# Means' rows by DMA, weight sums from step 16 on, and another place for the third product in a fused attention and feed-forward kernel

## The chip, the cores and the metric

The kernel runs as one launch on one core of a Trainium2 chip. A core has TensorE (PE in the profile; PEld is its weight load), VectorE (DVE), ScalarE (ACT), GpSimd (POOL) and SyncE (SP), which here issues every DMA. Each engine works through its own instructions in the order in which the program was written and waits on semaphores for the others. The metric is the device time of one execution in microseconds. Before the change it is 620.76 us, the median of three runs (620.72 to 621.04).

## The reference, cut to what matters

```python
# attention: 4 batches, 8 heads, 768 positions, 64 values a head; blocks of 32, window of 16
k_sum = k.reshape(B, H, nb, 32, D).max(axis=3)        # maxima of the keys of a block
v_sum = v.reshape(B, H, nb, 32, D).mean(axis=3)       # means of the values of a block
scores = concat(where(|i-j| < 16, q k^T / 8, -1e9), q k_sum^T / 8 + log(32))
x = softmax(scores) @ concat(v, v_sum)                 # 3072 tokens x 512
# feed-forward
h = x @ w_in                                           # 512 -> 2048
g = h * tanh(softplus(h))                              # Mish
out = g @ w_out                                        # 2048 -> 512
```

Inputs and output are float32.

## The kernel before

The kernel fuses both. Tokens go in six groups of 512 (g = 0 to 5), the hidden width in 16 slices of 128 (fc), so there are 96 steps (g, fc), numbered i = 16 g + fc. A matrix product in float32 is made of three products of rounded parts (upper x upper, upper x lower, lower x upper), so each weight and each activation exists as an upper and a lower part; the split is an upper copy on ACT (`ah`, L532) and a subtraction on DVE (`al`, L534).

**Attention** is done in 48 units (c, hp): 256 queries of one pair of heads. A unit has scores on PE (`att_scores`, L359), maxima on DVE (`att_maxima`, L380), exponentials on ACT (L393), divisors on DVE (L407, L408), the normalization on POOL (L412), a transpose on PE (L418) with a copy by ACT (L422), the product with the values on PE (L444) and, for later groups, a copy of the result by ACT into `x_blocks` (L483). For each unit SP loads the queries and keys into `qk` (L319) and the values into `vw` (L335). Both hold room for 24 rows or columns of block summaries: POOL copies the key maxima into `qk` (L324) and the value means into the last 24 rows of `vw`, four times side by side (L336). The maxima and means of a batch are made on DVE (`key_summary` L284, `value_means` L309) from sources which SP loads (L243, L247), and the means are laid out by a small DMA (`value_summary`, L315).

**Steps 0 to 18** are written out by hand as a list of words (`order`): `ph16` is the first layer's product of step 16, `po15` the second layer's of step 15, `al14` the lower part of step 14, `oc0` the copy of two of group 0's four finished output blocks from PSUM, and so on. In this stretch the weights are loaded as well and turned into float32 parts: five DVE instructions (L176 to L197) and two ACT instructions for each piece of 128 x 1024.

**Steps 19 to 31** run in a loop. Beside the steps, DVE makes what the last four groups need: there the first layer takes seven products for two slices instead of eight, and the factors are sums and differences of quarters of the weights. `weight_sums` puts them into a list of waiting DVE work: for pair p of slices `first_sums(p)` (L743 to L746, L733, L734) and `second_sums(p)` (L752, L733, L734), both in a work area called `results`, from which SP sends the parts to DRAM (`w_sums`, L721). `fill(us)` hands DVE as much of the waiting work as fits. Before the change pair 0 is made at the end of step 19, and pairs 1 to 5 from step 20 to 29, a half at each step. The same area is where ACT and DVE put finished output blocks (`ff_store`, L563), which SP stores (L564).

**Steps 32 to 63** go in pairs (`ff_in_pair`): the seven products 1 to 7 (six matmuls of 256 columns each, L806) into two PSUM tiles, `one` and `two`; `chain` is the left half of `one`, `other` the left half of `two`. Between the products ACT copies intermediate sums out (L813, L818, L819, L823), DVE adds (L816, L824, L831), and at the end ACT applies Mish (L829, L830, L832). The order on PE is: products 1, 2, 5, 6; half of the second layer of the pair before; product 7; the other half; products 4 and 3. `chain` holds product 1, then 6, 7 and 4 on top of one another; ACT copies it out after 1, after 6 and after 7. `other` holds product 5, which L819 copies out, and then product 3 is added on top of it. DVE adds the second layer's weight sums in the same stretch (L768 to L777). `load_sums` brings the sums of the pair after next from DRAM (L793, 1024 KB and 768 KB). The batch's maxima and means for the last batch are made after a pair's odd step, in `loads`.

**Steps 64 to 95** use the seven products in both layers and no attention.

Of the kernel before, what the change touches and what calls it, by code (L numbers as in the profile page):

```python
# [9 lines left out]
F32 = mybir.dt.float32  # L10
# [10 lines left out]
P = 128  # L21
# [36 lines left out]
MORE = (3.0, 2.5, 2.0, 3.0)  # L58
# [15 lines left out]
def fused_kernel(ctx: ExitStack, tc: tile.TileContext, q0, qk, kt, v0, vw, vs, w_in, w_out, out):  # L74
# [477 lines left out]
    stores = []  # L552

# [4 lines left out]
    def ff_store(g, *tokens):  # L558
        if not res:
            res.append(stage_words("results"))  # L560
        for t in tokens:
            o = res[0].rearrange("p (t f) -> p t f", t=TG // P)[:, t, :]
# [6 lines left out]


# [54 lines left out]
    def summary_of(name):  # L625
# [18 lines left out]
        "lvw": of_unit(att_load_values),  # L644
    }

# [18 lines left out]
        G15 al15 T16 ph17 pc17 al14 lqk19 kc19 X17 pc16 mi16 po14 po15 xh17 ah16 mi17 ah17 ph18 al16 oc0 oc1 mi18 X16  # L665
# [27 lines left out]
    dram = ctx.enter_context(tc.tile_pool(name="dram", bufs=1, space=bass.MemoryType.DRAM))  # L693
    kept = [dram.tile([P, 2, 7, CH], F32, name=f"w_sums_{p}") for p in range(NFC // 2)]
    kept_out = [dram.tile([P, 2, 3 * CH], F32, name=f"w_out_sums_{p}") for p in range(NFC // 2)]
# [5 lines left out]
    area = res[0]  # L701

    def home(p):
        k = 2 * p
        name, k = ("w_early", k) if k < EARLY else ("w_late", k - EARLY)
        t = grounds[name]
        n = t.shape[1] // 2
        return [t[:, part * n + k * WP:part * n + (k + 2) * WP] for part in range(2)]

    unsent = []  # L710

    def send():
        while unsent:
            unsent.pop(0)()

    def quarters(t):
        return t.rearrange("p (b f) -> p b f", f=CH)

    def keep(p, part, first, t):
        n = t.shape[1]  # L720
        unsent.append(lambda: nc.sync.dma_start(kept[p][:, part, first:first + n, :], t.bitcast(F32)))  # L721
        if p > 5:
            send()

    def keep_blocks(p):
        for part, t in enumerate(home(p)):
            for first, blocks_ in ((0, quarters(t[:, :2 * CH])), (2, quarters(t[:, 3 * CH:]))):
                keep(p, part, first, blocks_)

    def split_sums(p, first, whole, upper):  # L730
        whole = quarters(whole)
        hi, lo = upper.bitcast(F32R), whole.bitcast(F32R)
        return [(0.45, lambda: nc.vector.tensor_copy(hi, whole)),  # L733
                (0.7, lambda: nc.vector.tensor_sub(lo, whole, hi.bitcast(F32))),  # L734
                (0, lambda: (keep(p, 0, first, upper), keep(p, 1, first, whole)))]

    def first_sums(p):

        hi, lo = home(p)
        w, t = area[:, :2 * WP], area[:, 2 * WP:3 * WP]  # L740
        a11, a12, a21, a22 = (w[:, k * CH:(k + 1) * CH] for k in range(4))
        s1, s2 = t[:, :CH], t[:, CH:]
        return [(0, send), (1.25, lambda: nc.vector.tensor_add(w, hi.bitcast(F32), lo.bitcast(F32))),  # L743
                (0.45, lambda: nc.vector.tensor_add(s1, a21, a22)),
                (0.45, lambda: nc.vector.tensor_sub(s2, s1, a11)),
                (0.45, lambda: nc.vector.tensor_sub(a22, a12, s2))] + split_sums(  # L746
                    p, 3, t, quarters(area[:, 3 * WP:]))

    def second_sums(p):
        w = area[:, :2 * WP]  # L750
        a11, a21 = w[:, :CH], w[:, WP:3 * CH]
        made = [(0.45, lambda: nc.vector.tensor_sub(a21, a11, a21))]  # L752
        return made + split_sums(p, 5, w[:, WP:], quarters(w[:, :WP]))
# [9 lines left out]
    def out_sums(p):  # L763
        k = p % 2 if p < 5 else 0
        w = area[:, k * 2 * WP:(k + 1) * 2 * WP]
# [6 lines left out]
        hi = grounds["w_late"][:, (1 + k) * 4 * WP:][:, :2 * WP] if p < 5 else area[:, 2 * WP:].bitcast(F32R)  # L772
# [93 lines left out]
    def loads(i):  # L866
# [7 lines left out]
        for f, b, hp in sorted(chain.get(i, ()), key=in_order):  # L874
            f(b, hp)

# [460 lines left out]
```

## Time and profile before

| | |
|---|---|
| median of three runs | 620.76 us (620.72 to 621.04) |
| profiled execution, its own time | 620.96 us |
| span of its instructions | 619.0 us |
| mean granted TensorE clock | 0.996 |
| PE busy | 595.2 us (96%) |
| DVE busy | 461.1 us (74%) |
| ACT busy | 389.6 us (63%) |
| POOL busy | 114.6 us (19%) |
| DMA | 158.75 MB, mean 256 GB/s |

The span is the time from the first to the last instruction that the profile holds; the execution's own time holds 1.96 us more. Busy is the time in which an engine had an instruction under way. Numbers before an instruction are microseconds from the span's start; in brackets behind it stands the idle time of its engine just before it and who ended that.

### The profile page before, as it was taken

The page shows a single profiled execution, that of the slowest core. Times are in us where ns is not written, and L with a number is a line of the kernel's source. Part 1 is how long each engine was busy: PE and PEld are TensorE (multiplying, and loading weights), DVE is VectorE, ACT ScalarE, POOL GpSimd, SP SyncE. Part 2 cuts the span into 40 slices and gives each one's busy share as a digit, 9 for nine tenths or more (in the row PEclk, how much of TensorE's full clock was granted, in tenths as well). Part 3 has the DMA queues.
Part 4 walks back from the last instruction along what each step waited for, and adds up shares of the span by engine and source line. Part 5 has one row for each costly group of instructions (what it writes and reads, how often), then busy time and mean ns, then how long its engine had stood idle before and what let it go on. Part 6 is the DMA issues. An engine that isn't in the chain of part 4 may idle for free.

```text
span 619.0 us, 13932 instructions
## 1 busy us (share of the span) xinstructions
PE 595.2 (96%) x5142; PEld 527.4 (85%) x5142; DVE 461.1 (74%) x1158; ACT 389.6 (63%) x990; POOL 114.6 (19%) x159
## 2 busy tenths in 40 slices
PE   3899999999999998999999999999999999999997
PEld 3787777778788887888888889888889999999997
DVE  3999999995489758668695466888668777675564
ACT  3987576776446635577858785776446566755662
POOL 3642212322023112122222231322000000000000
PEclk9899999999999999999999999999999999999999
DMA  9977567661388888599988868686869989898853
GB/s 274 252 242 268 192 199 246 204 208 47 123 272 281 265 285 296 180 360 333 370 264 284 280 214 294 237 289 238 297 244 342 301 291 318 278 316 290 292 185 105
DMA packets 66644, 158.75 MB, mean 256 GB/s; under 512 B 9616, under 2 KB 18832, under 8 KB 66576
## 3 DMA queue, kind: packets, MB, share of 16 engines
q1 hardware_dynamic: 66576, 157.85, 75.5%
q8 instruction: 41, 0.67, 0.5%
q14 instruction: 27, 0.22, 0.1%
HBM read 130.42 MB, written 27.26 MB: 255 GB/s over the span
## 4 chain that ended last, share of the span: by engine, by line
PE 54%; DVE 18%; ACT 7%; DMA 7%; issue 2%; SPq 1%; POOL 0%; DVEq 0%; POOLq 0%; ACTq 0%
PE po L544 13%; PE m L1010 12%; PE inner L1112 12%; PE ph L806 9%; PE ph L516 3%; DMA vsum<-vs 3%; DMA qk<-qk 2%; ACT pr L393 2%; DVE al L534 2%; PE x_ps L444 2%; ACT L393 1%; PE pt_ps L418 1%; PE sc L359 1%; DVE w L180 1%; DMA w_sums<-results 1%
## 5 line engine op out<-in xcount | busy, mean ns | idle before, releaser
L412 POOL TENSOR_TENSOR pr<-pr,rs 128x480 f32<-128x480 f32 x48 | 58.7, 1224 | 258.0 <-DVE rs L408 216.6
L393 ACT ACTIVATE pr<-pr,nm 128x120 f32<-128x120 f32 x192 | 73.6, 386 | 18.7 <-DVE nm L380 18.5
L544 PE MATMUL po<-w_early_out_hi,al 128*128 128x512 f32 x160 | 62.7, 392 | 2.3 <-DVE al L534 2.3
L544 PE MATMUL po<-w_early_out_hi,ah 128*128 128x512 f32 x160 | 64.2, 401 | 0.0
L544 PE MATMUL po<-w_early_out_lo,ah 128*128 128x512 f32 x160 | 62.2, 389 | 0.0
L516 PE MATMUL ph<-xh,w_early_in 128*128 128x512 f32 x160 | 52.0, 391 | 0.0
L806 PE MATMUL ph<-xh,w_early_in 128*128 128x256 f32 x272 | 50.9, 279 | 0.7 <-ACT x_blocks L483 0.4
L1112 PE MATMUL inner<-xh,w_early_in 128*128 128x256 f32 x240 | 49.2, 279 | 0.0
L806 PEld LDWEIGHTS ph<-xh,w_early_in 128*128 128x128 f32 x272 | 42.7, 187 | 2.1 <-ACT h L813 0.8
L534 DVE TENSOR_TENSOR al<-h,ah 128x512 fp32r<-128x512 f32 x32 | 22.4, 709 | 26.0 <-ACT ah L532 26.0
L1112 PEld LDWEIGHTS inner<-xh,w_early_in 128*128 128x128 f32 x240 | 39.5, 187 | 0.1
L544 PE MATMUL po<-w_late_out_hi,ah 128*128 128x512 f32 x96 | 38.8, 404 | 0.0
L544 PEld LDWEIGHTS po<-w_early_out_hi,al 128*128 128x128 f32 x160 | 30.1, 188 | 9.0 <-DVE al L534 4.5
L380 DVE CUSTOM_DVE_ANT_0 pr<-sc,base 128x120 f32<-128x120 f32 x128 | 31.3, 276 | 8.6 <-PE sc L359 8.6
L544 PE MATMUL po<-w_late_out_lo,ah 128*128 128x512 f32 x96 | 37.5, 390 | 0.1
L806 PE MATMUL ph<-xl,w_early_in 128*128 128x256 f32 x136 | 37.4, 275 | 0.0
L336 POOL COPY vw<-vm 24x512 f32<-24x512 f32 x40 | 31.8, 817 | 29.7 <-PE x_ps L444 15.2
L544 PE MATMUL po<-w_late_out_hi,al 128*128 128x512 f32 x96 | 37.2, 388 | 0.0
L523 ACT ACTIVATE a<-ph 128x512 f32<-128x512 f32 x32 | 19.0, 599 | 28.0 <-PE ph L516 27.2
L393 ACT ACTIVATION_READ_ACCUMULATOR pr<-pr,nm 128x1 f32 x192 | 36.3, 189 | 0.0
L544 PEld LDWEIGHTS po<-w_early_out_hi,ah 128*128 128x128 f32 x160 | 30.0, 188 | 6.5 <-issue 1.6
L516 PEld LDWEIGHTS ph<-xh,w_early_in 128*128 128x128 f32 x160 | 30.0, 188 | 6.1
(269 smaller groups left out, 1754.1 us busy)
## 6 DMA issues: line engine op xcount, KB each, us to landing
w_early_in<-w_sums SPq DMA_DIRECT2D x32, 1024.0 KB, 7.5
w_early_in<-w_sums SPq DMA_DIRECT2D x32, 768.0 KB, 9.1
qk<-qk SPq DMA_DIRECT2D x40, 496.0 KB, 7.4
w<-w_in SPq DMA_DIRECT2D x16, 512.0 KB, 5.1
w<-w_out SPq DMA_DIRECT2D x16, 512.0 KB, 4.0
w_sums<-results SPq DMA_DIRECT2D x32, 256.0 KB, 3.0
vw<-vw SPq DMA_DIRECT2D x40, 192.0 KB, 3.9
w_late_in<-w_out_sums SPq DMA_DIRECT2D x25, 256.0 KB, 3.2
```

The source lines that it names most:

```text
L336: nc.gpsimd.tensor_copy(vwt[KW:KA], summary[b, hp][1].unsqueeze(1).broadcast_to([NB, NQ, P]))
L380: nc.vector.tensor_tensor_reduce(out=pr[:, j, :], in0=ps[h][:, at + pair * KA:at + (pair + 1) * KA], in1=m, scale=-SCALE, scalar=-NEG, op0 ...
L393: nc.scalar.activation(pr[:, s, :], pr[:, s, :], AF.Exp, scale=-1.0, bias=nm[:, s:s + 1], accum_out=sm[:, s:s + 1])
L412: nc.gpsimd.tensor_mul(u["p"], u["p"], u["r"].unsqueeze(2).broadcast_to([P, NQ, KA]))
L444: nc.tensor.matmul(x, u["v"][0:rows, s, d], pt, start=(c >= CG), stop=(c >= CG or s == NQ - 1))
L516: nc.tensor.matmul(turned(ph), w[:, cc * P:(cc + 1) * P], turned(x[:, cc, :]), start=(cc == 0 and n == 0), stop=(cc == NCC - 1 and n == 2))
L523: nc.scalar.activation(a, st[g, fc], AF.Mish)
L534: return lambda: nc.vector.tensor_sub(al, a, ah.bitcast(F32))
L544: nc.tensor.matmul(turned(po[g][t]), a[:, tok], turned(w), start=(fc == 0 and n == 0), stop=(fc == NFC - 1 and n == 2))
L806: nc.tensor.matmul(turned(ps), w_[:, a * P:(a + 1) * P], turned(x[:, a, :]), start=(begins and a == 0 and n == 0), stop=(a == 1 and n == 2 ...
L1010: nc.tensor.matmul(turned(ps), a_[:, tok], turned(w_), start=(begins and n == 0), stop=(n == 2), skip_group_check=True)
L1112: nc.tensor.matmul(turned(ps), w_[:, a * P:(a + 1) * P], turned(x[:, a, :]), start=(begins and a == 0 and n == 0), stop=(a == 1 and n == 2 ...
```

## The change

1. The means' rows of `vw` are written by a DMA on SP's queue instead of a copy on POOL.
2. The weight sums of pair 0 are made in the written order, as the words `W0a` (behind `al14`) and `W0b` (behind `po15`); those of pairs 1 to 5 come two steps earlier each (at the ends of steps 18 to 27). Their helper functions move up in the file unchanged, and the work area is fetched when first asked for. The first two loads of sums are issued at steps 25 and 30 instead of 25 and 27.
3. In `ff_in_pair` product 3 stands next to product 7, its addition next to the addition of 7, and the Mish of the first slice comes first.
4. For the last batch, maxima and means are made in the middle of the next pair, ahead of the filled-in work there, which gets 1 us less in such a pair.
5. `load_sums` of the pair after next is cut in two: products 1, 2, 4, 5 where it was, products 6, 7, 3 behind the loads of queries and keys.
6. In pairs without scores the third and fourth share of filled-in work are swapped.

```diff
-MORE = (3.0, 2.5, 2.0, 3.0)
+MORE = (3.0, 2.5, 3.0, 2.0)
...
-        nc.gpsimd.tensor_copy(vwt[KW:KA], summary[b, hp][1].unsqueeze(1).broadcast_to([NB, NQ, P]))
+        nc.sync.dma_start(vwt[KW:KA], summary[b, hp][1].unsqueeze(1).broadcast_to([NB, NQ, P]))
...
+    def sums_now(name):
+        p, second = int(name[:-1]), name[-1] == "b"
+        if not second:
+            keep_blocks(p)
+        for _, f in (second_sums if second else first_sums)(p):
+            f()
+        send()
...
-        G15 al15 T16 ph17 pc17 al14 lqk19 kc19 X17 pc16 mi16 po14 po15 xh17 ah16 mi17 ah17 ph18 al16 oc0 oc1 mi18 X16
+        G15 al15 T16 ph17 pc17 al14 W0a lqk19 kc19 X17 pc16 mi16 po14 po15 W0b xh17 ah16 mi17 ah17 ph18 al16 oc0 oc1 mi18 X16
...
-    def load_sums(pair):
+    def load_sums(pair, parts=(slice(0, 4), slice(4, 7))):
         if pair < (NG - WHOLE) * NFC // 2:
-            for some in (slice(0, 4), slice(4, 7)):
+            for some in parts:
...
         product(7, chain)
+        product(3, other)
         nc.scalar.copy(second[:, low], chain)
         nc.vector.tensor_add(second[:, high], second[:, low], second[:, high])
+        nc.vector.tensor_add(first_[:, high], other, first_[:, high])
         spread[1]()
         between[1]()
         product(4, chain)
-        product(3, other)
+        nc.scalar.activation(first_, first_, AF.Mish)
+        nc.scalar.activation(second[:, low], chain, AF.Mish)
         nc.scalar.activation(second[:, high], second[:, high], AF.Mish)
-        nc.scalar.activation(second[:, low], chain, AF.Mish)
-        nc.vector.tensor_add(first_[:, high], other, first_[:, high])
-        nc.scalar.activation(first_, first_, AF.Mish)
...
-    def loads(i):
+    def loads(i, pair=None):
...
-        for f, b, hp in sorted(chain.get(i, ()), key=in_order):
+        if pair is not None:
+            load_sums(pair, [slice(4, 7)])
+        if i < whole_steps:
+            summaries(i)
+
+    def summaries(i):
+        some = sorted(chain.pop(i, ()), key=in_order)
+        for f, b, hp in some:
             f(b, hp)
+        return some
...
-    order_of_sums = {20 + k: (k // 2 + 1, k % 2) for k in range(10)}
+    order_of_sums = {18 + k: (k // 2 + 1, k % 2) for k in range(10)}
...
-        if i == done:
-            keep_blocks(0)
-            put_first(0, first_sums(0) + second_sums(0))
...
+    weight_sums(done - 1)
+    fill(8)
...
-        if whole_steps - i in (7, 5):
+        if i in (25, 30):
             send()
-            load_sums(3 - (whole_steps - i) // 2)
+            load_sums(int(i == 30))
...
-                   [lambda: (second_exponents(0), fill(slots[0], i + 0.3)), lambda: (second_exponents(1), norms(i), fill(slots[1], i + 0.6))])
+                   [lambda: (second_exponents(0), fill(slots[0] - (summaries(i - 1) + summaries(i) != []), i + 0.3)), lambda: (second_exponents(1), norms(i), fill(slots[1], i + 0.6))])
...
-        load_sums(pair + 2)
+        load_sums(pair + 2, [slice(0, 4)])
...
-        loads(i + 1)
+        loads(i + 1, pair + 2)
```

## Rows read from the trace of the kernel before

**Rows 1.** Busy time in two stretches: us, then PE, PEld, DVE, ACT, POOL (instructions).
```profile
40.00:134.00 94.00, 89.56 (x637) 70.80 (x634) 90.79 (x159) 63.54 (x121) 24.60 (x20) 1.00 0.63 205
134.00:245.00 111.00, 111.00 (x746) 90.84 (x745) 79.42 (x198) 59.34 (x145) 22.33 (x27) 1.00 0.68 224
```

**Rows 2.** Waits of PE and PEld, whole span: us in total, times, longest.
```profile
PE pt_ps L418 <- POOL pr L412: 4.9, 3, 1.9
...
PEld ph L806 <- ACT h L813: 0.8, 3, 0.3
...
PEld ph L806 <- ACT x_blocks L483: 0.6, 1, 0.6
```

**Rows 3.** Timeline, POOL's first, second and last L336 of 40 to 134, DVE beside them.
```profile
55.07 1.49 POOL L336 COPY vw<-vm 24x512 f32<-24x512 f32 x1
56.01 1.10 DVE L534 TENSOR_TENSOR al<-a,ah 128x512 fp32r<-128x512 f32 x1
...
70.32 0.96 POOL L336 COPY vw<-vm 24x512 f32<-24x512 f32 x1
69.33 1.48 DVE L176 TENSOR_SCALAR w<-w 128x1024 uint32<-128x1024 uint32 x1
70.73 1.09 DVE L534 TENSOR_TENSOR al<-a,ah 128x512 fp32r<-128x512 f32 x1
...
128.19 2.44 POOL L336 COPY vw<-vm 24x512 f32<-24x512 f32 x2 [7.28 <-PE ph L516]
130.08 1.12 DVE L176 TENSOR_SCALAR w<-w 128x1024 uint32<-128x1024 uint32 x1
```

**Rows 4.** Source line L176: minimum, median and maximum of its sixteen instructions in ns.
```profile
L176 DVE TENSOR_SCALAR w<-w x16: 680/691/1483, 17.2 to 139.8; 128x1024 uint32<-128x1024 uint32 x16
```

**Rows 5.** DMA issues: tiles, count, KB each, median us to landing.
```profile
w_sums<-results SPq DMA_DIRECT2D x32, 256.0 KB, 3.0
```

**Rows 6.** Timeline from 154 to 162 us, DVE, ACT, PE.
```profile
154.27 0.69 DVE L534 TENSOR_TENSOR al<-a,ah 128x512 fp32r<-128x512 f32 x1 [4.64 <-ACT ah L532]
...
155.91 0.58 ACT L563 COPY results<-po 128x512 f32<-128x512 f32 x1
...
161.18 0.49 PE L544 MATMUL po<-w_early_out_hi,ah 128*128 128x512 f32 x1
```

**Rows 7.** Timeline from 172 to 179 us, DVE: pair 0's sums, first and last instruction.
```profile
172.96 1.21 DVE L743 TENSOR_TENSOR results<-w_early_in 128x1024 f32<-128x1024 f32 x1
...
178.10 0.69 DVE L734 TENSOR_TENSOR results<-results 128x512 fp32r<-128x512 f32 x1
```

**Rows 8.** Timeline from 236 to 248 us, DVE and PE.
```profile
236.62 1.23 DVE L743 TENSOR_TENSOR results<-w_late_in 128x1024 f32<-128x1024 f32 x1 [1.61 <-DMA w_sums<-results]
...
240.20 0.28 DVE L380 CUSTOM_DVE_ANT_0 pr<-sc,first 128x120 f32<-128x120 f32 x1
...
247.72 0.65 PE L418 MATMUL pt_ps<-ident,pr 128*120 128x128 f32 x4 [1.76 <-POOL pr L412]
```

**Rows 9.** Timeline from 254 to 256 us, DVE and PE.
```profile
254.18 0.42 DVE L816 TENSOR_TENSOR h<-ph,h 128x256 f32<-128x256 f32 x1
...
255.33 1.71 PE L806 MATMUL ph<-w_early_in 128*128 128x256 f32 x12 [0.79 <-ACT h L823]
```

**Rows 10.** Timeline round 266 us: DVE, ACT and PE in the second pair.
```profile
264.22 0.92 DVE L284 TENSOR_REDUCE spare<-ks 128x24 f32<-128x768 f32 x1
...
266.70 0.37 ACT L819 COPY h<-ph 128x256 f32<-128x256 f32 x1 [1.26 <-DVE h L816]
...
266.23 0.89 PE L806 MATMUL ph<-w_early_in 128*128 128x256 f32 x6
```

**Rows 11.** Timeline round 458 us, ACT and PE: the last pair.
```profile
458.13 0.37 ACT L819 COPY h<-ph 128x256 f32<-128x256 f32 x1 [0.54 <-DVE h L816]
...
458.37 0.84 PE L806 MATMUL ph<-w_early_in 128*128 128x256 f32 x6
```

**Rows 12.** Timeline at 430 us, ACT.
```profile
430.94 0.63 ACT L832 ACTIVATE h<-h 128x512 f32<-128x512 f32 x1 [3.74 <-DVE h L831]
```

More of the change, by code (lines that the diff above doesn't have):

```diff
@@ L552, in fused_kernel @@
     stores = []
+    unsent = []
     def store():
@@ L558, in ff_store @@
     def ff_store(g, *tokens):
-        if not res:
-            res.append(stage_words("results"))
         for t in tokens:
-            o = res[0].rearrange("p (t f) -> p t f", t=TG // P)[:, t, :]
+            o = area().rearrange("p (t f) -> p t f", t=TG // P)[:, t, :]
             (nc.vector.tensor_copy if t % 2 else nc.scalar.copy)(o, po[g][t])
@@ L568, in ff_store, with area, home @@
                 put_out()
+    dram = ctx.enter_context(tc.tile_pool(name="dram", bufs=1, space=bass.MemoryType.DRAM))
+    kept = [dram.tile([P, 2, 7, CH], F32, name=f"w_sums_{p}") for p in range(NFC // 2)]
+    kept_out = [dram.tile([P, 2, 3 * CH], F32, name=f"w_out_sums_{p}") for p in range(NFC // 2)]
+    def area():
+        if not res:
+            res.append(stage_words("results"))
+        return res[0]
+    def home(p):
+        k = 2 * p
+        name, k = ("w_early", k) if k < EARLY else ("w_late", k - EARLY)
+        t = grounds[name]
+        n = t.shape[1] // 2
+        return [t[:, part * n + k * WP:part * n + (k + 2) * WP] for part in range(2)]
@@ new lines, in send, with quarters, keep, keep_blocks @@
+    def send():
+        while unsent:
+            unsent.pop(0)()
+    def quarters(t):
+        return t.rearrange("p (b f) -> p b f", f=CH)
+    def keep(p, part, first, t):
+        n = t.shape[1]
+        unsent.append(lambda: nc.sync.dma_start(kept[p][:, part, first:first + n, :], t.bitcast(F32)))
+        if p > 5:
+            send()
+    def keep_blocks(p):
+        for part, t in enumerate(home(p)):
+            for first, blocks_ in ((0, quarters(t[:, :2 * CH])), (2, quarters(t[:, 3 * CH:]))):
+                keep(p, part, first, blocks_)
@@ new lines, in split_sums, with first_sums @@
+    def split_sums(p, first, whole, upper):
+        whole = quarters(whole)
+        hi, lo = upper.bitcast(F32R), whole.bitcast(F32R)
+        return [(0.45, lambda: nc.vector.tensor_copy(hi, whole)),
+                (0.7, lambda: nc.vector.tensor_sub(lo, whole, hi.bitcast(F32))),
+                (0, lambda: (keep(p, 0, first, upper), keep(p, 1, first, whole)))]
+    def first_sums(p):
+        hi, lo = home(p)
+        w, t = area()[:, :2 * WP], area()[:, 2 * WP:3 * WP]
+        a11, a12, a21, a22 = (w[:, k * CH:(k + 1) * CH] for k in range(4))
+        s1, s2 = t[:, :CH], t[:, CH:]
+        return [(0, send), (1.25, lambda: nc.vector.tensor_add(w, hi.bitcast(F32), lo.bitcast(F32))),
+                (0.45, lambda: nc.vector.tensor_add(s1, a21, a22)),
+                (0.45, lambda: nc.vector.tensor_sub(s2, s1, a11)),
+                (0.45, lambda: nc.vector.tensor_sub(a22, a12, s2))] + split_sums(
+                    p, 3, t, quarters(area()[:, 3 * WP:]))
@@ L571, in fused_kernel, with second_sums @@
+    def second_sums(p):
+        w = area()[:, :2 * WP]
+        a11, a21 = w[:, :CH], w[:, WP:3 * CH]
+        made = [(0.45, lambda: nc.vector.tensor_sub(a21, a11, a21))]
+        return made + split_sums(p, 5, w[:, WP:], quarters(w[:, :WP]))
     todo = [(c, hp) for c in range(NCH) for hp in range(HP)]
@@ L643, in fused_kernel @@
         "dv": of_batch(value_summary), "lqk": of_unit(att_queries), "kc": of_unit(att_key_summary),
-        "lvw": of_unit(att_load_values),
+        "lvw": of_unit(att_load_values), "W": lambda name: sums_now(name),
     }
+    def sums_now(name):
[4 more added lines that the diff above has]
+            f()
+        send()
     order = """
@@ L700, in fused_kernel @@
     maxima_home.append(spare[:, CH:])
[L701 to L753, printed above, removed]
     def both_layers(k, part):
@@ L764, in out_sums @@
         k = p % 2 if p < 5 else 0
-        w = area[:, k * 2 * WP:(k + 1) * 2 * WP]
+        w = area()[:, k * 2 * WP:(k + 1) * 2 * WP]
         b11, b12, b21, b22 = (w[:, k * CH:(k + 1) * CH] for k in range(4))
@@ L771, in out_sums @@
             (b11, b12, b11), (b12, b22, b12), (b22, b22, b11), (b21, b21, b22))]
-        hi = grounds["w_late"][:, (1 + k) * 4 * WP:][:, :2 * WP] if p < 5 else area[:, 2 * WP:].bitcast(F32R)
+        hi = grounds["w_late"][:, (1 + k) * 4 * WP:][:, :2 * WP] if p < 5 else area()[:, 2 * WP:].bitcast(F32R)
         lo = w.bitcast(F32R)
@@ L970, in fused_kernel @@
         weight_sums(i)
-        if i == done or i in range(20, 29):
+        if i in order_of_sums:
             fill(8)
-        if whole_steps - i in (7, 5):
+        if i in (25, 30):
             send()
-            load_sums(3 - (whole_steps - i) // 2)
+            load_sums(int(i == 30))
     late_exponents = []
```

3 lines of the change are left out of this document (removed).

## The prediction

> **What bounds the kernel now.** I read the busy times by stretch first, then who made TensorE wait, then the timeline at each such wait. The reader is to see that TensorE sets the time nearly everywhere and that only its idle microseconds can be won. From 134 to 245 it is busy in all 111.00 us [rows 1]: an edit there gains nothing by itself. From 40 to 134 it idles for 94.00 - 89.56 = 4.44 us, while DVE idles for 94.00 - 90.79 = 3.21 us only: DVE, which turns the weights into parts, leads there. Later the idle time lies in a few places. One transpose at 247.72 waited 1.76 us for POOL [rows 8] (it is most of POOL's entry among the waits, whose longest is 1.9 [rows 2]); one group of products at 255.33 waited 0.79 us for an ACT copy [rows 9]; in the pairs, weight loads waited 0.8 us for the copy L813 and 0.6 us for the copy into `x_blocks` [rows 2]. These and the 4.44 us make about 8.4 us, the restarts of PE behind each wait not counted. That is all that this change can reach; the stretch of steps 64 to 95 it leaves alone.
>
> **Part 1, the means' rows.** Removed: forty POOL copies. What they cost is not POOL's time but DVE's. At 70.32 one copy of 0.96 us stands beside 0.49 us of an L176 that took 1.48 us, where the median is 0.69 [rows 3, 4], and beside an L534 that took 1.09 instead of the 0.69 that it takes with POOL idle [rows 3, 6]. Shared by overlap that is 0.79 x 0.49 / 1.48 = 0.26, and 0.40, so 0.66 us of DVE. At 55.07 the L534 beside the copy lost 0.41, at 128.19 the L176 beside two copies lost 1.12 - 0.69 = 0.43 [rows 3, 4]. That is 1.5 us over four copies; the stretch has six (these, and two at 88 and 115), so 1.5 x 6 / 4 = 2.25 us. DVE leads there and TensorE has 4.44 us of waiting to lose, so I take 2.2 us on the path. Bounds: 0, if DVE's time goes into its own waits, to 4.4, all of TensorE's idle time [rows 1].
>
> The Trainium skill (GPSIMD Engine Reference, section 1, Specifications) says that POOL shares its SBUF interfaces with VectorE and that DVE instructions in a two-port mode or with two SBUF inputs contend. L176 and L534 are of these two kinds and the rows agree. Taken to its end, with DVE held for the copy's whole length, the rule would give 0.96 us a copy where the row at 70.32 gives 0.66, so six copies would give 5.8 us by it; no more than 4.4 could reach the path.
>
> Added: forty DMAs on SP's queue, each behind the load of `vw`. The trace has no such DMA; the nearest row is a small transfer that lands after 3.0 us [rows 5]. A unit's rows are used one turn later, so I take 0 (if no turn lay between, up to 3.0 us each). SP now also waits in line until the means have landed; behind it stand the loads of sums and queries, both used a pair later.
>
> **Part 2, weight sums.** They move; their number is the same. Pair 0 takes 178.10 + 0.69 - 172.96 = 5.83 us of DVE [rows 7]. It now starts at 149.6, where DVE idles for 4.64 us [rows 6], and ends by 155.5; the lower part of step 16 comes 1.2 us later than at 154.27 and is first used at 161.18 [rows 6], so it costs nothing. What is new is a wait: the finished output blocks of group 0 go into the same work area. ACT's copy at 155.91 [rows 6] and DVE's must now wait until SP has sent pair 0's sums, 155.5 plus some 0.6 of issue plus 3.0 of landing [rows 5], so until 159.1; two copies of 0.58 [rows 6] end at 160.3, and the second layer of step 16, which needs the freed PSUM, starts at 161.18. About 0.9 us is left, so I take 0.4 us of loss on average. Bounds: 0, to 3.0 if the transfer takes twice the median.
>
> At the other end the sums of pair 5 leave steps 28 and 29. There DVE made its first half at 236.62, behind a DMA wait of 1.61 us, so the maxima of the units scored at step 29 began at 240.20 [rows 8]; exponentials, normalization and transpose stood behind them, and the transpose at 247.72 is where TensorE paid. With the half (236.62 to 240.20, 3.6 us) and its wait gone the maxima come some 5 us earlier, more than 1.76: gain 1.76 us (0 to 1.9). DVE's backlog reaches into the first pair too: L816 came at 254.18, the copies behind it on ACT followed, and the products waited 0.79 us [rows 9]. Two second-half instructions of pair 5 stood before it. That wait goes as well: 0.79 us (0 to 0.9); part 3 alone would also take most of it.
>
> **Part 3, product 3 by product 7.** The matmuls are the same. `chain` must be copied out after product 7 before product 4 writes it; now product 3 (six matmuls, half of a group of 12) stands between as well, about 0.7 us more room. DVE's addition L831 no longer stands behind filled-in work, and so ACT's Mish L832 does not: at 430.94 ACT had idled for 3.74 us for it [rows 12]. What stood behind ACT then were the copies L813 and `x_blocks`, for which TensorE waited 0.8 + 0.6 us [rows 2]: gain 1.4 us (0.6 to 1.9, the restarts of PE counted). The new wait is product 3's: L819 must have read `other`. In the last pair L819 ends at 458.50, and product 7, begun at 458.37, ends about 0.7 later: 0.55 us to spare [rows 11]. In the second pair it ends at 267.07 and product 7 at about 266.95, so 0.1 us late [rows 10]; but DVE's L284 of 0.92 us stood ahead of it [rows 10], and that is moved by part 4. I take 0.
>
> **Parts 4 to 6** move DVE and SP work inside a pair, and DVE has room there: 0 each, from -0.5 to 0.5.
>
> **Sum.** 2.2 + 1.76 + 0.79 + 1.4 - 0.4 = 5.75 us off the profiled execution's own 620.96 (span 619.0 and 1.96 around it): 615.2. The median of the runs is 0.2 lower: **615.0 us**.
>
> **Rivals.**
> *DVE's gain stays on DVE.* In the stretch up to 134 DVE also waits for ACT and DMAs, and POOL's normalizations still run beside it. Then 2.2 is missing: 617.2. Against it: DVE idles for 3.4% only.
> *Group 0's results wait for the sums.* If SP's queue, which stands at each sum until DVE has made it, or the transfer takes 3 us longer than I say, the second layer of step 16 starts up to 2.1 us late (3.0 less 0.9), and all behind it, as TensorE has no idle time up to 245 [rows 1]: 615.0 - 0.4 + 2.1 = 616.7.
> *The waits only change place* (the maxima at step 29 wait for another DMA, the copies for another DVE instruction): within 0.2%, about 620.5. For it: the wait at 236.62 was a DMA's too.
> *Slower: product 3 waits for L819 in every pair.* The room is 0.55 us in the last pair and -0.1 in the second [rows 10, 11]. If L816, and L819 behind it, come 1 us later than now, as they would with the maxima or means still ahead of them or a DMA wait in DVE's queue, a pair loses 0.4 to 1.1 us. From about 0.42 us a pair on, 7.1 us in the 17 pairs, the gain of 5.75 is more than gone: 622.1. Against it: the work that made L816 late moves behind it.
>
> **How the numbers follow.** My forecast has 0.57, DVE's gain staying 0.12, the results' wait 0.13, no change 0.09, slower 0.09. Faster by over 0.2% (1.2 us, what a measurement of this kernel can tell from no change) is 0.57 + 0.12 + 0.13 = 0.82, within it 0.09, slower 0.09. The forecast's own range goes from 620.76 less the upper bounds (4.4 + 1.9 + 0.9 + 1.9 = 9.1), 611.7, to 618.2, where only parts 2 and 3's sure waits (1.76 + 0.79) are won. To leave no more than 2 in 10 out I reach up to 619.3, and down to 611.3.
>
> **What would show it.** Right: TensorE idle from 40 to 134 near 2.2 us instead of 4.4; no wait of a transpose near 247 and none at 255; L176 near its median all through; no TensorE wait for `x_blocks` or L813; L832 never waiting for L831 for microseconds. Wrong: a gap of TensorE before the second layer of step 16 (about 158), short gaps before product 3 in most pairs, new waits for `vw` rows at the product with the values.

## The result and the profile after

The changed kernel takes 612.51 us (median of 5 runs, 611.74 to 614.98) against 620.72 for the kernel before on the same chip (620.39 to 621.04): the ratio is 0.9878, with a 95% interval from 0.9856 to 0.9900. The forecast was 615.0 us with a range from 611.3 to 619.3. The time lies inside it, and the direction is as forecast, but 2.5 us more were won than forecast. The profiled execution took 612.42 us, its span is 610.7.

The busy times of after by stretch answer to [rows 1] (the same columns: PE, PEld, DVE, ACT, POOL, the clock, DMA's share, GB/s). The stretches are shifted by what had been won up to there.

```profile
40.00:131.00 91.00, 88.58 (x639) 71.46 (x634) 88.65 (x163) 64.10 (x121) 16.32 (x13) 1.00 0.68 220
131.00:240.00 109.00, 109.00 (x737) 89.19 (x736) 84.60 (x208) 60.47 (x147) 15.76 (x20) 1.00 0.75 250
240.00:250.00 10.00, 10.00 (x69) 9.13 (x68) 2.27 (x5) 3.67 (x8) 0.00 (x0) 1.00 0.12 49
250.00:275.00 25.00, 25.00 (x236) 22.14 (x235) 14.36 (x58) 20.09 (x58) 3.61 (x6) 1.00 0.85 306
395.00:430.00 35.00, 34.92 (x329) 31.21 (x329) 30.58 (x90) 23.06 (x65) 5.61 (x6) 1.00 0.82 277
```

TensorE idles 91.00 - 88.58 = 2.42 us in the first stretch, where it idled 4.44 [rows 1]. From 131 to 275 it never idles, and from 395 to 430 for 0.08 us. DVE's 2.27 us in 240 to 250 show how far its backlog of [rows 8, 9] has gone. TensorE's waits in after answer to [rows 2]:

```profile
PE pt_ps L418 <- POOL pr L412: 1.7, 1, 1.7
PE x_ps L444 <- DMA vw<-vm: 1.4, 1, 1.4
PE sc L363 <- DVE rs L407: 1.0, 1, 1.0
PE ph L516 <- DVE w_late_in L197: 0.5, 1, 0.5
PE sc L359 <- POOL qk L324: 0.4, 1, 0.4
PE po L544 <- DVE al L534: 0.4, 1, 0.4
```

Those for POOL that are left lie at 13 and 15 us. New is a wait of 1.4 us for the rows that now come by DMA. What follows compares like with like: TensorE has 5142 matmul records in every kernel here, so the time from one record's start to another's can be set side by side. The table, worked out from these starts, holds the microseconds between records 448, 1137, 1872, 2018, 2173, 3322, 3655 and 5141, which in after lie near 35, 131, 240, 255, 275, 395, 431 and 606 us; at each of them every kernel has the same matmul. It leaves out the first 35 us, in which the same program takes from 34.0 to 37.1 us in the profiles of eight kernels that differ from after only behind them, and 35.2 and 39.0 us in before and in before with part 2. On the chips of the experiments the kernel before spread from 618.4 to 625.1 us, so 1 or 2 us are read from the table and not from the whole times, though each row is one execution alone, and those of the blocks early, of part 2 and of parts 1, 2 are the slowest of their kernels' runs.

```
profiled kernel            35-131 131-240 240-255 255-275 275-395 395-431 431-606   sum
before                      99.47  108.87   18.53   20.15  120.06   37.49  174.69  579.26
after                       96.14  108.84   15.52   19.51  119.95   35.82  174.81  570.59
POOL copies back (1 undone) 99.21  108.87   15.52   19.51  119.94   36.26  174.57  573.88
sums late (2 undone)        96.34  112.03   20.52   19.51  119.94   35.82  174.63  578.79
product 3 late (3 undone)   96.36  108.84   15.51   19.50  120.53   37.09  174.71  572.53
means at step ends (4 und.) 96.40  108.84   15.52   19.90  119.94   35.82  174.71  571.12
sums loaded whole (5 und.)  96.33  108.84   15.52   20.78  119.95   35.81  174.75  571.98
before + part 1             96.40  110.13   17.93   20.74  120.05   36.66  174.62  576.53
before + part 2             99.16  108.86   15.51   21.58  120.03   37.50  174.71  577.36
before + parts 1, 2         96.38  108.84   15.51   23.35  120.02   36.62  174.75  575.46
before, copies twice       102.98  109.83   19.23   20.51  120.32   37.60  174.82  585.29
rows earlier                96.39  108.84   15.52   19.51  119.94   35.82  174.75  570.77
sums late, blocks early     97.50  112.43   20.61   19.51  119.95   35.80  174.75  580.56
only pair 0's sums early    96.13  108.84   20.42   19.51  119.95   35.80  174.81  575.47
```

After wins 579.26 - 570.59 = 8.67 us: 3.33 up to 131, 3.01 from 240 to 255, 0.64 in the second pair (255 to 275), 1.67 from 395 to 431, 0.02 elsewhere. How far two executions of the same program can lie apart shows in two places of the table. Up to 131 us the blocks early run after's program and took 97.50 us, where after and seven other kernels that run it there took 96.13 to 96.40; behind a wait of 2.27 us at 72.24 TensorE's granted clock was 0.63 until 76. And from 131 to 240 us part 1 alone and the sums late run the same instructions in the same order on every engine, in 110.13 and 112.03 us.

### The profile page after: what moved, and what is told of

It reads as the page before. It is cut to its first block, busy times and chain, and to the rows that moved or that the text cites. A ratio compares the mean times of both kernels' runs of the same rounds, so it can differ in the third digit from the quotient of the medians.

```text
span 610.7 us, 13901 instructions
## 1 busy us (share of the span) xinstructions
PE 592.3 (97%) x5142; PEld 527.6 (86%) x5142; DVE 452.3 (74%) x1158; ACT 386.7 (63%) x990; POOL 82.1 (13%) x119
## 4 chain that ended last, share of the span: by engine, by line
PE 79%; DVE 7%; issue 1%; DMA 1%; ACT 0%; SPq 0%; DVEq 0%
PE po L544 24%; PE ph L816 13%; PE m L1027 12%; PE inner L1129 12%; PE ph L516 9%; PE x_ps L444 3%; PE sc L359 3%; PE pt_ps L418 3%; DVE al L534 1%; DVE w L180 1%; DVE w L176 1%; DVE w_f L184 1%; DMA qk<-qk 1%; DVE w_early_out_lo L197 1%; DVE w_f L189 1%
## 5 line engine op out<-in xcount | busy, mean ns | idle before, releaser
L412 POOL TENSOR_TENSOR pr<-pr,rs 128x480 f32<-128x480 f32 x48 | 57.6, 1202 | 288.1 <-DVE rs L408 258.8
L816 PE MATMUL ph<-xh,w_early_in 128*128 128x256 f32 x272 | 49.6, 277 | 0.0
L534 DVE TENSOR_TENSOR al<-h,ah 128x512 fp32r<-128x512 f32 x32 | 21.8, 689 | 29.7 <-ACT ah L532 29.7
L816 PEld LDWEIGHTS ph<-xh,w_early_in 128*128 128x128 f32 x272 | 42.4, 187 | 0.5
L523 ACT ACTIVATE a<-ph 128x512 f32<-128x512 f32 x32 | 19.0, 598 | 31.6 <-PE ph L516 31.1
L422 ACT COPY pt<-pt_ps 120x512 f32<-120x512 f32 x48 | 26.3, 590 | 17.9 <-PE pt_ps L418 13.9
L544 PEld LDWEIGHTS po<-w_early_out_lo,ah 128*128 128x128 f32 x160 | 30.0, 188 | 6.2
```

The costliest lines, as they stand in the source:

```text
L412: nc.gpsimd.tensor_mul(u["p"], u["p"], u["r"].unsqueeze(2).broadcast_to([P, NQ, KA]))
L422: nc.scalar.copy(pt.rearrange("p s q -> p (s q)"), u["t"][:KA, :])
L523: nc.scalar.activation(a, st[g, fc], AF.Mish)
L534: return lambda: nc.vector.tensor_sub(al, a, ah.bitcast(F32))
L544: nc.tensor.matmul(turned(po[g][t]), a[:, tok], turned(w), start=(fc == 0 and n == 0), stop=(fc == NFC - 1 and n == 2))
L816: nc.tensor.matmul(turned(ps), w_[:, a * P:(a + 1) * P], turned(x[:, a, :]), start=(begins and a == 0 and n == 0), stop=(a == 1 and n == 2 ...
```

## The experiments

**Part 1 undone in after, and part 1 alone in before.** One line each, the second the reverse of the first:

```
-        nc.sync.dma_start(vwt[KW:KA], summary[b, hp][1].unsqueeze(1).broadcast_to([NB, NQ, P]))
+        nc.gpsimd.tensor_copy(vwt[KW:KA], summary[b, hp][1].unsqueeze(1).broadcast_to([NB, NQ, P]))
```

> After with part 1 alone undone: POOL copies the means' rows again, everything else stays. Theory (POOL's copies slow DVE, which leads from 40 to 131 us): the early stage falls back by about 3 us, TensorE idles some 4.4 us there again, L176 and L534 beside the copies take 0.3 to 0.8 us more than their medians, and the rest of the span is as in after: 615 to 616 us against 612.5. Rival (the early gain is from the changed order of the DMAs or from somewhere else in the change): within 1 us of 612.5, and TensorE's idle time up to 131 us near 2.4.

> The kernel before with part 1 alone done: the means' rows by DMA. Theory: some 3 us from the stretch up to 134 us and nothing behind it: 617 to 618 us against 620.7; the waits of TensorE at 247 and 255 us stay. Rival (what DVE wins stays on DVE unless its later work moves too): 620 to 621. Rival (POOL's copies also cost the late pairs): 616 or less.

Measured: 617.01 us, ratio to before 0.9940 (0.9922 to 0.9957), and 617.61, ratio 0.9950 (0.9933 to 0.9967). With the copies back, the stretch to 131 us loses 99.21 - 96.14 = 3.07 us, and everything behind it but 0.44 us stays won. TensorE idles 4.14 us in it, and beside the copies at 55 and 70 us DVE has the lengths of [rows 3] again (columns: start, duration, engine, line). The copy at 26.87 us has no DVE instruction beside it:

```profile
40.00:134.00 94.00, 89.86 (x639) 70.86 (x638) 91.02 (x158) 63.86 (x122) 24.74 (x21) 1.00 0.64 210
...
26.87 0.61 POOL L336 COPY vw<-vm 24x512 f32<-24x512 f32 x1
...
55.67 1.49 POOL L336 COPY vw<-vm 24x512 f32<-24x512 f32 x1
56.61 1.10 DVE L534 TENSOR_TENSOR al<-a,ah 128x512 fp32r<-128x512 f32 x1
...
70.96 0.96 POOL L336 COPY vw<-vm 24x512 f32<-24x512 f32 x1
71.36 1.09 DVE L534 TENSOR_TENSOR al<-a,ah 128x512 fp32r<-128x512 f32 x1
```

Of the 3.07 us, some 2.9 lie at nine matmuls that wait for DVE, their restarts counted, and 0.6 at one behind ACT's L523, which waits for DVE's L534; the wait for the rows is 0.5 us shorter than in after. So the early gain is the copies', as the theory has it, and comes by way of DVE. Part 1 alone wins the same 3.07 us there, but 1.26 us are lost again before 240 and 0.59 in the second pair, against 0.60 won between them (and 0.83 in the late pairs). TensorE is 4.3 us earlier at 131 us than in the profile of before, but DVE's first instructions for pairs 3 to 5 are only 1.9, 3.0 and 2.8 us earlier. TensorE's waits there:

```profile
239.76 0.49 PE L544 MATMUL po<-w_late_out_hi,al 128*128 128x512 f32 x1 [1.03 <-DVE al L534]
244.20 0.66 PE L418 MATMUL pt_ps<-ident,pr 128*120 128x128 f32 x4 [1.23 <-POOL pr L412]
251.74 1.72 PE L806 MATMUL ph<-w_early_in 128*128 128x256 f32 x12 [0.71 <-ACT h L823]
268.80 0.44 PE L359 MATMUL sc<-qk 64*64 64x120 f32 x8 [0.66 <-POOL qk L324]
```

The first wait is one that before did not have.

**The copies doubled.** Before, with `for _ in range(2):` ahead of the copy.

> The kernel before with every POOL copy of the means' rows made twice, one behind the other (the second writes the same values). Theory (it is time beside DVE that costs): 1.5 to 3.5 us slower than before, 622 to 624, from more DVE instructions beside copies in the stretch up to 134 us, and TensorE's idle time there 6 to 8 us with DVE named as what it waits for. Rival (the copies cost by what waits behind them on POOL, or by TensorE's wait for the rows): the same time within 0.5 us but for waits that name POOL, about 1 us at the one place at 71 us where TensorE already waits for a copy.

Measured: 629.19 us, ratio 1.0141 (1.0122 to 1.0160), more than either theory expected. DVE is busy 92.39 us from 40 to 137 where 40 to 134 had 90.79 [rows 1], and its instructions, set side by side one by one, take 1.6 us longer; that part stands. But TensorE's waits for POOL grew too (here every line behind 336 is one later):

```profile
PE pt_ps L419 <- POOL pr L413: 8.5, 4, 3.0
...
PE x_ps L445 <- POOL vw L337: 2.0, 1, 2.0
```

They are 4.9 in [rows 2], and for the rows 0.93 in before. POOL's queue was thus close to being a bound as well: one more copy per unit, and the normalizations behind it were late at 44 us (a wait of 1.94 us that before did not have) and at 254 us (2.98, where before had the 1.76 of [rows 8]). Behind the wait for the rows, at 74.55 us, TensorE's clock fell too (last section). The run doesn't separate these causes; that before lost its time to 131 us beside DVE rests on part 1 undone, where the one wait for POOL's rows, 0.97 us, is shorter than after's 1.44 for the DMA.

**Part 2 undone in after.** The sums go back to the steps from 19 on (`W0a` and `W0b` out of the order, each later half two steps later, the first two loads of sums at steps 25 and 27):

```
-    order_of_sums = {18 + k: (k // 2 + 1, k % 2) for k in range(10)}
+    order_of_sums = {20 + k: (k // 2 + 1, k % 2) for k in range(10)}
...
+        if i == done:
+            keep_blocks(0)
+            put_first(0, first_sums(0) + second_sums(0))
```

> After with part 2 alone undone: pair 0's sums wait for step 19, each later half stands two steps later as before, and the first two loads of sums go out where they did. Theory: the wait of the transpose near 242 us returns (1.8 us and its restart, 2.0 in all) and most of the wait of the first pair's products (0.8 to 1.2), unless part 3 covers it: 614.5 to 615.7 us against 612.5. Rival (the other parts already free DVE and POOL there): within 0.5 us of 612.5, no such wait. What the results' wait for pair 0's sums costs, if anything, is won back: up to 0.4 us.

Measured: 619.35 us, ratio 0.9963 (0.9941 to 0.9985). The loss is far above the 2.0 to 3.2 us of the theory: 3.19 us from 131 to 240 and 5.00 from 240 to 255. TensorE's waits:

```profile
218.70 0.65 PE L418 MATMUL pt_ps<-ident,pr 128*120 128x128 f32 x4 [1.16 <-POOL pr L412]
242.42 0.50 PE L544 MATMUL po<-w_late_out_hi,al 128*128 128x512 f32 x1 [1.53 <-DVE al L534]
246.86 0.65 PE L418 MATMUL pt_ps<-ident,pr 128*120 128x128 f32 x4 [1.22 <-POOL pr L412]
254.13 0.99 PE L816 MATMUL ph<-w_early_in 128*128 128x256 f32 x6 [1.80 <-ACT h L829]
```

The last is product 3, which waits for L829, and L829 for DVE's L826 (ACT idled 3.05 us ahead of it), which stood behind pair 5's second half. Without part 2, then, the slower rival's mechanism comes true in the first pair. The granted clock fell behind that wait, to 0.71 from 254.1 to 260.0, so 1.5 of the 5.00 us are slower matmuls. And DVE's sums stand where they stood before, though TensorE is 3 us earlier (first instructions of pairs 3 to 5; pair 5's was at 236.62 in [rows 8]):

```profile
206.82 1.23 DVE L617 TENSOR_TENSOR results<-w_early_in 128x1024 f32<-128x1024 f32 x1 [2.87 <-DMA w_sums<-results]
...
223.62 1.23 DVE L617 TENSOR_TENSOR results<-w_early_in 128x1024 f32<-128x1024 f32 x1 [2.43 <-DMA w_sums<-results]
...
236.47 1.23 DVE L617 TENSOR_TENSOR results<-w_late_in 128x1024 f32<-128x1024 f32 x1 [1.59 <-DMA w_sums<-results]
```

How much is lost differs from run to run, though. Part 1 alone, the same program up to 249 us, lost 1.29 us against after from 131 to 240 where this run lost 3.19; it had no wait at 218, and its DVE waited less for pair 3's place (L743 is L617 here):

```profile
204.20 1.23 DVE L743 TENSOR_TENSOR results<-w_early_in 128x1024 f32<-128x1024 f32 x1 [0.77 <-DMA w_sums<-results]
```

**Is it the amount of transfers?** The kernel of the late sums, with twelve stores of plain blocks (pairs 1 to 3) sent at 139.7 us instead of between the sums:

```
+        "K": lambda name: (keep_blocks(int(name)), send()),
...
-... ph18 al16 oc0 ...
+... ph18 K1 K2 K3 al16 oc0 ...
```

> The kernel of the late sums (after with part 2 undone) with one thing more: the plain blocks of pairs 1 to 3, which go to memory beside the sums, are sent at the end of the weight stage, when the queues move 90 to 130 GB/s, and not between the sums, where they move 270 to 320. DVE's work and its order stay as in that kernel. Theory (the sums are paced by their transfers, since the next sum waits until the last one has left the work area): DVE's waits of 2.4 to 2.9 us ahead of the first halves of pairs 3 and 4 shrink below 1 us, and of the 8 us that the late sums lost against after 3 or more come back: 613 to 616.5 us. Rival (it is DVE's own work that is late, whatever the transfers do): the same as with the late sums, 618 to 620.

Measured: 619.52 us, ratio 0.9974 (0.9946 to 1.0002), as with the late sums. DMA's share from 190 to 210 fell from 0.72 to 0.59, and yet DVE waited for the same stores, here for pair 3 (2.48 us for pair 4):

```profile
209.40 1.23 DVE L617 TENSOR_TENSOR results<-w_early_in 128x1024 f32<-128x1024 f32 x1 [2.10 <-DMA w_sums<-results]
```

My theory of a row of sums paced by how much is moved fell in this run: DVE waits until the half before has left the work area, also with less moved beside it.

**Which of part 2's moves counts?** After, with pair 0 early but pairs 1 to 5 two steps later (`order_of_sums` from 20, the call of `weight_sums` ahead of the loop gone).

> After with only pair 0's sums early: those of pairs 1 to 5 stand at their old steps, two later. Theory (transfers pace the sums, so that what counts is when the row of sums begins): pair 0's transfers are out of the way, the waits of DVE for transfers shrink, but the first half of pair 5 stands ahead of the maxima of step 29 again, 3.6 us of DVE: the transpose near 242 us waits 0 to 1.5 us: 613 to 614.5 us. Rival (the place of pair 5's half decides alone): the loss of the late sums between 131 and 256 us, 5 us or more, returns: 617 to 620.

Measured: 619.24 us, ratio 0.9957 (0.9932 to 0.9983). From 131 to 240 nothing is lost, so pair 0's early place alone saves what the late sums lose there: 3.19 us against that run, 1.29 against part 1 alone. (The second load of sums, which part 2 moves as well, goes out behind 230 us in all three.) From 240 to 255, 4.90 us are lost, as the rival said, but not at the transpose:

```profile
247.35 0.42 DVE L626 TENSOR_TENSOR results<-results 128x256 f32<-128x256 f32 x1
247.80 0.43 DVE L607 CAST results<-results 128x512 fp32r<-128x512 f32 x1
248.27 0.69 DVE L608 TENSOR_TENSOR results<-results 128x512 fp32r<-128x512 f32 x1
248.88 1.29 DVE L534 TENSOR_TENSOR al<-a,ah 128x512 fp32r<-128x512 f32 x2
...
249.65 0.37 ACT L823 COPY h<-ph 128x256 f32<-128x256 f32 x1 [4.00 <-DVE al L534]
...
250.07 0.38 PE L816 MATMUL ph<-xh,w_early_in 128*128 128x256 f32 x1 [3.06 <-ACT h L823]
```

Pair 5's second half (1.5 us) stands ahead of L534. The pair's `h` takes the buffer (tag `t`, two of them) of the activations that L534 still has to read. So ACT's copy out of `chain`, and behind it product 6, wait for DVE's queue. Of the 4.90 us this wait and its restart make 3.2, and slower matmuls behind it, at a lower clock (last section), 1.7. That the clock falls in every execution isn't shown: the twelve runs lie from 614.87 to 621.60 us.

**Part 2 alone, and parts 1 and 2, in before.** The edits are those of part 2 and part 1, applied to before.

> The kernel before with part 2 alone done: weight sums from step 16 on. My working gave it 1.76 at the transpose and 0.79 in the first pair, less 0.4, so 2.2 us; with the restarts that after shows, up to 3.2: 617.3 to 618.6 us against 620.7, the stretch up to 131 us as before and the late pairs as before. Rival (the first pair's wait for the copies needs part 3): the wait near 255 us stays, 618.5 to 619.3. Rival (the sums only pay once part 1 has brought the weight stage forward): under 1 us.

> The kernel before with parts 1 and 2 done, without the rest. Theory (part 1's early gain comes through to the end only with the sums moved; the pairs' order is a matter of its own): 3.1 us from the stretch to 131 and about 3 from 240 to 256, and the late pairs keep their waits: 614 to 615 us. Rival (the parts don't need each other): the sum of the two alone, 620.7 less 3.4 less what part 2 alone wins, 614.5 to 615 as well, but then with 1.2 us lost again between 131 and 275 as in part 1 alone.

Measured: 618.79 us, ratio 0.9970 (0.9950 to 0.9990), and 615.58, ratio 0.9906 (0.9882 to 0.9931). Part 2 alone wins 3.02 us from 240 to 255, the whole of it without part 3, so its rival fell; but it loses 1.43 in the second pair. With part 1 as well, that loss is 3.20 us, of which against after's records 1.6 are slower matmuls behind the wait, at half the clock; but what part 1 alone lost before 240 us is not lost, as the theory said. TensorE and POOL of the two-part kernel in the second pair:

```profile
267.70 2.03 PE L359 MATMUL sc<-qk 64*64 64x120 f32 x32 [1.79 <-POOL qk L324]
...
266.96 0.69 POOL L324 COPY qk<-km 128x96 f32<-128x96 f32 x1 [1.75 <-DMA qk<-qk]
```

A load of sums of seven blocks (1.8 MB) stands ahead of the queries on SP's queue, and a first pair that comes earlier leaves them less time; the next experiment takes this up.

**Part 5 undone in after.** `load_sums(pair + 2)` whole again, `loads(i + 1)` without the second half.

> After with part 5 alone undone: each pair's sums are loaded by two DMAs one behind the other again, ahead of the queries. Theory (the 0.6 us won in the second pair come from the queries' load, which no longer stands behind the second half of the sums): 612.8 to 613.3 us, with a short wait for the scores' queries or their key rows in the second pair. Rival: no difference within 0.3 us, and the second pair as in after, since its waits went with the earlier sums of part 2.

Measured: 615.08 us, ratio 0.9891 (0.9855 to 0.9927). 1.27 us are lost in the second pair, and only there: TensorE waits 0.88 us for L324, POOL's key copy L324 0.71 and 1.25 for the queries (in after not at all). My working had part 5 at nothing.

**Part 4 undone in after.** `loads` calls `summaries(i)` in every step, the middle of the pair does not.

> After with part 4 alone undone: the last batch's maxima and means stand at the ends of steps again instead of in the middle of a pair. Theory (my working took part 4 as worth nothing): within 0.5 us of 612.5. Rival (with product 3 next to product 7 the copy that frees its bank comes late where a reduction of 0.9 us stands ahead on DVE): TensorE waits for L829 in the second pair and in those that hold the last batch's work, 0.1 to 1.0 us in each of up to six pairs: 613 to 615.

Measured: 613.20 us, ratio 0.9867 (0.9842 to 0.9892). 0.39 us are lost in the second pair, part of it a product's wait for L829 (0.17 us with its restart), and none elsewhere: the first theory, with the rival's mechanism at one place. By its ratio the kernel can't be told from after (0.9878).

**Part 3 undone in after.** Product 3 stands behind product 4, and the copies, additions and activations in the old order.

> After with part 3 alone undone: product 3 behind product 4 again and the copies, additions and activations in the old order. Theory: the waits of TensorE for the copies of a pair and for the copy into the x blocks return between 395 and 430 us, 1.4 to 1.9 us; with part 2 in place little of the first pair's wait at 255: 613.9 to 614.8 us. Rival (these waits came from the means and maxima, which part 4 moves): within 0.5 us of 612.5. Rival (the first pair's wait depends on part 3): 615 to 615.5.

Measured: 614.32 us, ratio 0.9882 (0.9855 to 0.9909). From 275 to 431, 1.85 us are lost, in waits for L823 (361.85, 399.42, 414.22), `x_blocks` (409.54) and L833. Nothing is lost from 240 to 255, so part 3 has no share in that wait.

**A version that might be better.** After waited at 70.86 for rows whose DMA went out at 66.73:

```profile
66.73 0.81 SPq L336 DMA_DIRECT2D vw<-vm  x1
...
70.86 0.69 PE L444 MATMUL x_ps<-pt,vw 120*64 120x64 f32 x16 [1.44 <-DMA vw<-vm]
```

In the order, `lvw10` goes from behind `ls15` to behind `lt12`.

> After with one load moved: the loads of unit 10's values and means' rows go out ahead of the loads of weight 6 and of a value source, just behind the value source of batch 12, so some 3 us earlier. In after TensorE waited 1.44 us at 70.86 us for these rows. Theory: this wait goes, of it 0.5 to 1.4 us reach the end (an ACT wait of 0.55 us lay just behind it in the kernel before and may come back): 611 to 612 against 612.5. Rival (the stretch is led by DVE, so TensorE only waits a little later for DVE): the same time within 0.3 us, and the waits at 86, 103 and 122 us grow by what was won.

Measured: 613.58 us, ratio 0.9883 (0.9867 to 0.9900). The wait for the rows is gone, and others stand in its place:

```profile
60.00 0.50 PE L544 MATMUL po<-w_early_out_hi,al 128*128 128x512 f32 x1 [0.20 <-DVE al L534]
70.46 0.69 PE L444 MATMUL x_ps<-pt,vw 120*64 120x64 f32 x16 [0.82 <-ACT a L523]
71.50 0.63 PE L418 MATMUL pt_ps<-ident,pr 128*120 128x128 f32 x4 [0.36 <-ACT a L523]
```

The stretch takes 96.39 us; after and seven other kernels with after's order there take 96.13 to 96.40. DVE leads it, and the rival holds: the new wait costs nothing that can be told from the spread. No kernel here is shown to be faster than after.

## Why the prediction came out right, step by step

- **Part 1, 2.2 us.** Right in mechanism, too small: 3.07 us by both experiments. The price of DVE's own time was near. Instruction by instruction, DVE's work from 36 to 135 us takes 2.4 us longer with the copies back than in after, and 2.0 of it lie in five instructions that start beside a copy, 0.35 to 0.42 us each. What the sum left out is what stands behind DVE: the restart of TensorE after each wait, and ACT. One row was misread. The L176 of 1.48 us at 70 us, of which the prediction charged 0.26 to the copy, takes as long in after, where no copy is left and the normalization L412 runs beside it; so the sign "L176 near its median all through" was wrong as well. The L534 behind it has its 0.68 us back:

```profile
68.37 1.48 DVE L176 TENSOR_SCALAR w<-w 128x1024 uint32<-128x1024 uint32 x1
69.77 0.68 DVE L534 TENSOR_TENSOR al<-a,ah 128x512 fp32r<-128x512 f32 x1
```

The Trainium skill (GPSIMD Engine Reference, section 1, Specifications) says that POOL shares its SBUF interfaces with VectorE and that DVE instructions in a two-port mode or with two SBUF inputs contend. The trace agrees: L534 took 0.41 us longer beside a copy. Taken to its end the rule gave 0.96 us a copy in the prediction, which was too much: that length is itself 0.35 us above the 0.61 of the copy with no DVE instruction beside it, so the copy had lost time as well.

- **Part 1's new DMAs, 0.** Right by themselves, though a wait of 1.44 us appears at one unit. What I left out is part 1's loss further on: without part 2, 1.25 us of its gain are gone by 275, as DVE's sums move less than TensorE does. The rival "DVE's gain stays on DVE" described something like that at the wrong place.

- **Group 0's results, -0.4.** The wait came as described (the copies of the output blocks wait 3.97 and 2.42 us for pair 0's store), and it cost nothing. DVE's copies end at 155.47 + 1.29 = 156.76, and the second layer of step 16 starts at 157.67 without a wait: 0.9 us to spare, the figure that the prediction had.

```profile
154.81 1.07 ACT L562 COPY results<-po 128x512 f32<-128x512 f32 x2 [2.42 <-DMA w_sums<-results]
...
155.47 1.29 DVE L562 COPY results<-po 128x512 f32<-128x512 f32 x2 [3.97 <-DMA w_sums<-results]
...
157.67 0.49 PE L544 MATMUL po<-w_early_out_hi,ah 128*128 128x512 f32 x1
```

- **The transpose and the first pair, 1.76 + 0.79.** Right; with the restarts behind the waits 3.0 us. A reading beside it was wrong: the 1.76 us are not most of POOL's 4.9 [rows 2], whose longest wait, 1.9, lies at 16 us and a third, 1.2, at 30 us; the term did not use this, its upper bound of 1.9 did. Wrong was that part 3 alone would take most of the second: with part 3 and without part 2, product 3 waited 1.80 us there. The term also priced part 2 against the kernel before alone, at 2.55 us. Undone in after it cost 8.2 us by the profiles, 3.2 up to 240 us, which pair 0's place saves, and 5.0 behind it, which the places of pairs 1 to 5 save, 1.5 of the 8.2 by a lower clock; and 6.2 by the medians (619.35 against the 613.20 of the means at step ends on the same chip). On top of part 1 alone it wins only 1.07 in the table (576.53 - 575.46), as the second pair needs part 5 as well.

- **Part 3, 1.4 us.** 1.85 when undone, 1.78 between before and after from 275 to 431. ACT's wait for L831 (L836 after) is not gone, as I had said, but 6.3 us in all with 2.1 the longest (14.7 with 3.7 before); that is not TensorE's. The slower rival's wait, product 3 for L829, is there once in after, 0.28 us on the weight load at 402.46: one of 17 pairs.

```profile
ACT h L840 <- DVE h L836: 6.3, 6, 2.1
...
402.46 0.77 PEld L816 LDWEIGHTS ph<-w_late_in,w_early_in 128*128 128x128 f32 x6 [0.28 <-ACT h L829]
```

- **Parts 4 to 6, 0 each.** This is the step that was off in kind: part 5 is worth 1.3 us and part 4 0.4 as the last ones undone, by the table. Before had short waits in the second pair, for POOL's normalization and for the key copy. Without part 5 the second pair takes 1.3 us more than in after, 2.1 more in before with part 2 alone, and 3.8 more with parts 1 and 2 (1.6 of it by the clock). I had counted part 5's DMAs but not what a pair that comes earlier asks of the queue. Part 6, the slots of filled-in work, was not run alone.

Against the sum of 5.75 us, after won 8.67: 1.1 more up to 131 us, 0.9 more from 240 to 255 (with the loss of 0.4 that did not come), 0.4 more in the late pairs, 0.6 in the second pair, and 0.1 less elsewhere. Every term came out at or above its forecast, so no error made up for another.

Undone one at a time the parts are worth 3.3, 8.2, 1.9, 0.5 and 1.4 us by the profiles, together 15.3, where all of them win 8.67. The medians say much the same: against the kernel nearest to after on the same chip (rows earlier, 613.58; means at step ends, 613.20), parts 1, 2, 3 and 5 undone cost 3.4, 6.2, 1.1 and 1.9 us, together 12.6.

Open remains why the late sums lost all of their 3 us between 191 and 207 us where part 1 alone, the same program, lost less. The store that DVE waited for at 206.82 had been issued by 201.40, 5.4 us earlier; in after the one for 217.60 by 214.79, 2.8 us earlier. The plain blocks alone don't decide it. Open, too, is how the 2.2 us of the second pair's loss with parts 1 and 2 that are not the clock's divide over parts 5 and 4.

## What to carry to other kernels

A gain early in a kernel arrives at the end only if the engines that feed the bounding one move forward with it: look along the trace for work that is held by transfers or by a fixed place in a queue, and price that part of a change against the kernel with the early gain, not against the kernel before. A copy on an idle engine is not free where it slows the engine that leads the stretch; compare the durations of one instruction form with and without it, copy by copy. A wait that the trace names may have another right behind it, as at 70 us here, and is then worth nothing. And before a stretch's difference between two profiles is put down to an edit, look for a kernel that runs the same program there: 1.9 us of the late sums' loss turned out to differ from run to run.

## What the runs showed of the hardware

TensorE's granted clock fell to 0.50 of full speed, its lower level of 1.2 GHz, behind some of its waits. In the kernel with only pair 0's sums early it had idled 3.0 us, in the one with parts 1 and 2 for 1.8 us in a stretch of 2.60 in which it was busy for 0.80, in the one with the copies doubled for 2.01 us; the columns are those of the first fence, the kernels in this order:

```profile
247.00:250.00 3.00, 0.01 (x1) 0.00 (x0) 2.93 (x6) 0.35 (x1) 0.00 (x0) 1.00 0.29 105
250.00:253.20 3.20, 3.13 (x12) 2.66 (x13) 0.50 (x2) 0.67 (x3) 0.00 (x0) 0.67 0.87 257
...
265.00:267.60 2.60, 0.80 (x6) 0.41 (x4) 0.86 (x2) 2.57 (x6) 0.85 (x2) 1.00 0.98 318
267.70:271.10 3.40, 3.40 (x35) 2.57 (x36) 1.20 (x11) 2.24 (x7) 0.27 (x1) 0.50 1.01 379
...
74.50:78.00 3.50, 3.45 (x24) 3.05 (x25) 3.46 (x4) 1.25 (x3) 0.00 (x0) 0.51 0.23 94
```

In the first kernel the 128x512 matmuls behind the wait start 0.43 us apart, where they start 0.23 apart elsewhere. The wait of 3.1 us and the slower matmuls behind it make up that kernel's 4.9. The length of the wait alone doesn't decide: behind the 1.76 us of [rows 8] the clock stayed at 1.00, and so it did behind the longest wait of the doubled copies, 2.98 us at 253.68 (1.00 up to 262).

DVE and POOL slowed each other in these runs: a copy of 24x512 f32 on POOL took 0.61 us with no DVE instruction beside it and 0.96 us at 70.96, and the DVE instruction that started beside it 1.09 instead of 0.68.

The issue of a means' rows DMA takes SP 0.83 us (median of forty), twice that of the four times larger load of `vw` ahead of it (0.44):

```profile
L336 SPq DMA_DIRECT2D vw<-vm x40: 800/834/1249, 24.7 to 423.3; - x40
...
L335 SPq DMA_DIRECT2D vw<-vw x40: 327/440/1249, 24.2 to 422.7; - x40
```
